# Score tiles of two and three PSUM banks by turns in a fused attention and expert-attention kernel

## The chip, the cores and the metric

The kernel runs on one NeuronCore of a Trainium2 chip. The metric is the device time of one execution in microseconds. The kernel before takes 320.8 us (median of three runs, 320.77 to 320.80). The profile is of one execution with a span of 319.3 us.

Engine names in the profile: PE is TensorE (PEld its weight loads), DVE is VectorE, ACT is ScalarE, POOL is GpSimd, SP issues the transfers.

## What is computed

An attention with a soft cap on its scores, then, on its output, an attention layer of four experts with a gate that picks two of them for each token. Cut to what matters:

```python
# B = 8 batches, 12 heads, S = 448 tokens, 64 columns per head
scores = q @ k.T / sqrt(64)
scores = cap * tanh(scores / cap)              # cap = 30
attn   = softmax(scores)
x      = (attn @ v), heads side by side        # (8, 448, 768)

for e in range(4):                             # experts, causal
    a_e  = softmax(causal(x @ wq[e] @ (x @ wk[e]).T / sqrt(64)))
    y_e  = a_e @ (x @ wv[e]) @ wo[e]
out = sum over the two best experts of a token (logits x @ w_gate) of weight * y_e
```

So each of the 8 x 12 heads has 448 x 448 scores that pass through a tanh and then an exp. Both run on ScalarE.

## The kernel before

Heads are worked on in 48 pairs. The scores of a pair lie transposed: keys on partitions, queries along the row. 448 keys are three blocks of 128 and a tail of 64; the tails of the two heads share one block, so a pair has seven blocks of 128 x 448 scores: one tail block, and three blocks for each head. The first 43 pairs are handled whole; the last five (the last pairs of the last batch) are handled in two halves of tokens ("A" of 256 and "B" of 192 tokens) so that the end of the last batch can overlap.

[...]one block fills one bank (448 of its 512 columns). Scores have two tiles of two banks, used by turns; everything else that TensorE writes (transposes, attention times values, projections, output) takes one of four single banks.

```python
ps_aux   = tile_pool(name="ps_aux", bufs=4, space=PSUM)      # single banks
ps_score = tile_pool(name="ps_score", bufs=2, space=PSUM)    # [128, 2, 512] f32 each
...
HALF = (1, 2, 2, 2)                    # blocks of a whole pair in its four tanh operations

def fill(p, i):                        # scores of part i of pair p, on TensorE
    qt, kt = qkt[p]
    sc = ps_score.tile([128, 2, 512], f32, name=f"s{i}_{p}", tag="score")
    if i == 0:                         # the tail block of both heads
        nc.tensor.matmul(sc[:, 0, 0:S], kt[:, 0:128], qt, start=True, stop=True)
    else:                              # block i of each head: 64 rows of the array each
        for g in range(2):
            r = slice(64 * g, 64 * (g + 1))
            nc.tensor.matmul(sc[:, g, 0:S], kt[r, 128 * i : 128 * (i + 1)], qt[r, :],
                             start=True, stop=True)
    score[(p, i)] = sc

def tanh(u, i):                        # ScalarE, from PSUM to y in SBUF (f16)
    ...
    nc.scalar.activation(dst, src, AF.Tanh, scale=isc / capf)

def expo(u):                           # ScalarE, the whole pair (7 * 448 columns) at once
    nc.scalar.activation(pt[:, 0:n], y.pop(u)[:, 0:n], AF.Exp, scale=capf)
```

The order on ScalarE is a fixed program. For pair i it is: first tanh of pair i, exp of pair i-1, then the other tanh operations of pair i. In some pairs the expert attention of an earlier batch adds two exps of its own ("X", names sB and pBs), which use score tiles too:

```python
XAT = [(3, 5)] * 5 + [(2, 4), (2, 3), (3, 4)]      # in which pairs of the next batch
for i, u in enumerate(UNITS):
    t = [("T", u, k) for k in range(2 if isinstance(u, tuple) else 4)]
    e = [("E", UNITS[i - 1])] if i else []
    x = [("X", *EXPB[i], g) ...] if i in EXPB else []
    if i in (1, 2):
        prog += e + t
    elif isinstance(u, tuple):                     # half pairs at the end
        prog += t[0:1] + e + x + t[1:]
    else:
        prog += t[0:1] + e + x[0:1] + t[1:2] + x[1:2] + t[2:4]
```

While the kernel is built, a small planner (`Plan`) goes through this program, keeps estimated clocks of PE, VectorE and ScalarE, and puts the other TensorE work between the score fills: transposes of q and k ("tr", tile tps), attention times values (pv), its transpose (xt, tile xtp), and for each batch the query and key projections (qps, kps), values (vps), expert attention (pvB), its transposes (otp) and output projections (wops). Its list `aux` has one entry per single bank: the time at which it comes free. Matrix multiplications without use ("dummy") fill gaps of TensorE in the first pairs.

At the end `last_batch` gives the score banks back, opens them as single banks (`ps_tail`, four), and orders what is left with a list scheduler (`Graph`) over both pools.

Of the kernel before, what the change touches and what calls it, by code (L numbers as in the profile page):

```python
# [10 lines left out]
f32 = mybir.dt.float32  # L11
f16 = mybir.dt.float16
AF = mybir.ActivationFunctionType
# [4 lines left out]
class Plan:  # L18
# [6 lines left out]
    def __init__(self):  # L25
        self.pe = self.dve = self.act = 0.0
        self.done = {}

        self.aux = [0.0] * 4
        self.opened = set()  # L30
        self.work = []

# [207 lines left out]
def kernel(  # L240
# [13 lines left out]
    nc = tc.nc  # L254

    B, H, S, Dh = q.shape
# [17 lines left out]
    xp = ctx.enter_context(tc.tile_pool(name="xp", bufs=2))  # L274
    bp = ctx.enter_context(tc.tile_pool(name="bp", bufs=2))
    outp = ctx.enter_context(tc.tile_pool(name="outp", bufs=8))
    ps_aux = ctx.enter_context(tc.tile_pool(name="ps_aux", bufs=4, space=bass.MemoryType.PSUM))
    scores = ctx.enter_context(ExitStack())
    ps_score = scores.enter_context(
        tc.tile_pool(name="ps_score", bufs=2, space=bass.MemoryType.PSUM)  # L280
    )

    ctx.enter_context(tc.manual_schedule())
# [154 lines left out]

    HALF = (1, 2, 2, 2)


    CUT = 256
# [4 lines left out]
    score = {}  # L449

    def fill_part(u, i):

        p, h = u
        qt, kt = qkt[p]
        x = slice(*TOK[h])
        n = x.stop - x.start
        sc = ps_score.tile([128, 2, 512], f32, name=f"s{i}{h}_{p}", tag="score")
# [12 lines left out]
    def fill(p, i):  # L470
        if isinstance(p, tuple):
            return fill_part(p, i)
        qt, kt = qkt[p]
        sc = ps_score.tile([128, 2, 512], f32, name=f"s{i}_{p}", tag="score")
        if i == 0:
            nc.tensor.matmul(sc[:, 0, 0:S], kt[:, 0:128], qt, start=True, stop=True)  # L476
        else:
            for g in range(2):
                r = slice(64 * g, 64 * (g + 1))
                nc.tensor.matmul(  # L480
                    sc[:, g, 0:S], kt[r, 128 * i : 128 * (i + 1)], qt[r, :],
                    start=True, stop=True,
                )
        score[(p, i)] = sc

    y = {}
# [2 lines left out]
    def tanh(u, i):  # L489
        p, h = u if isinstance(u, tuple) else (u, "")  # L490
        if i == 0:
            y[u] = actp.tile([128, 7 * S], f16, name=f"y{h}_{p}", tag="y", bufs=2)
        sc = score.pop((u, i))
        if not h:
            o, n = sum(HALF[0:i]), HALF[i]
            parts = [(o * S, sc[:, 0:n, 0:S], n)]
        else:
            n = TOK[h][1] - TOK[h][0]
            if i == 0:
                parts = [(0, sc[:, :, 0 : 2 * n], 2)]  # L500
            elif 2 * n == 512:
                parts = [(4 * n, sc.rearrange("p b n -> p (b n)")[:, 0 : 3 * n], 1)]
            else:
                parts = [(4 * n, sc[:, 0, 0 : 2 * n], 1), (6 * n, sc[:, 1, 0:n], 1)]
        for o, src, k in parts:
            w = src.shape[-1]
            dst = y[u][:, o : o + k * w]
            if k > 1 or len(src.shape) > 2:
                dst = dst.rearrange("p (k w) -> p k w", w=w)
            nc.scalar.activation(dst, src, AF.Tanh, scale=isc / capf)  # L510
# [8 lines left out]
    def prob(p, w, j, g):  # L519

        h = "AB"[w >= CUT]
        if (p, h) in pr:
            lo, hi = TOK[h]
            i = (4 if j == 0 else 4 + g + (j == 3) if j > 2 else j - 1 + 2 * g)
            o = (hi - lo) * i + w - lo
            return pr[p, h][:, o : o + 128]
        o = S * (0 if j == 0 else 2 * j - 1 + g) + w
        return pr[p][:, o : o + 128]

    xt = {}  # L530
# [96 lines left out]
    st = {b: {} for b in range(B)}  # L627
# [125 lines left out]
    def b_fill(b, r, g):  # L753
        s = st[b]
        qe = s["qe", r]
        ke = s["ke", r]
        sc = ps_score.tile([128, 1024], f32, name=f"sB{g}_{b}_{r}", tag="score")

        def block(e, o, ko, n, to):

            h = slice(64 * e, 64 * (e + 1))
            nc.tensor.matmul(  # L762
                sc[to : to + n, o : o + S - ko], ke[h, ko : ko + n], qe[h, ko:S], start=True,
                stop=True,
            )
# [136 lines left out]
    plan = Plan()  # L902
# [68 lines left out]
        loads += [("o", wo2[e // 2][e % 2 * Dh : (e % 2 + 1) * Dh, :], moe_wo[e])]  # L971


    XAT = [(3, 5)] * 5 + [(2, 4), (2, 3), (3, 4)]
    EXPB = {HP * (b + 1) + o: (b, r) for b in range(B) for r, o in enumerate(XAT[b])}

    prog = []
    for i, u in enumerate(UNITS):  # L980
        t = [("T", u, k) for k in range(2 if isinstance(u, tuple) else 4)]
        e = [("E", UNITS[i - 1])] if i else []
        x = [("X", *EXPB[i], g) for g in range(1 if i >= NP else 2)] if i in EXPB else []
        prog.append(("S", i))
        if i in (1, 2):
            prog += e + t
        elif isinstance(u, tuple):
            prog += t[0:1] + e + x + t[1:]
        else:
            prog += t[0:1] + e + x[0:1] + t[1:2] + x[1:2] + t[2:4]  # L990
    prog += [("S", len(UNITS)), ("E", UNITS[-1])]
    reads = [o for o in prog if o[0] in "TX"]
    where = [i for i, o in enumerate(prog) if o[0] in "TX"]
# [4 lines left out]
    def dur(o):  # L998
        if o[0] == "S":
            return 0.0  # L1000
        if o[0] == "X":
            return 0.7 if o[1] == B - 1 else 0.9
        n = S
        if isinstance(o[1], tuple):
            n = TOK[o[1][1]][1] - TOK[o[1][1]][0]
        if o[0] == "E":
            return 0.08 + 0.00084 * 7 * n
        if n < S:
            return 0.05 + 0.00084 * n * (4, 3)[o[2]] + 0.04 * (o[2] == 1 and n < 256)
        return 0.055 + 0.373 * HALF[o[2]]  # L1010

    def fill_dep(o):
        if o[0] == "T":
# [5 lines left out]
    def do_fill():  # L1019
        nonlocal nfill  # L1020
        o = reads[nfill]
        rel = ends[nfill - 2] + 0.15 if nfill >= 2 else 0.0
        cost = 0.36 if o[0] == "X" or o[2] or isinstance(o[1], tuple) else 0.19
# [15 lines left out]
    t = 0.0  # L1039
# [185 lines left out]


    def l_fill(b, r, _):
        sc = ps_score.tile([128, 2, 512], f32, name=f"sLA_{r}", tag="score")
        o = 0
        for _, k0, q0, q1 in BANKS["A", r][0]:  # L1230
            for e in range(2):
                h = slice(64 * e, 64 * (e + 1))
                nc.tensor.matmul(
                    sc[:, e, o : o + q1 - q0], part_of(1, r, h, k0, k0 + 128),
                    part_of(0, r, h, q0, q1), start=True, stop=True,
                )
            o += q1 - q0
        st[b]["sc", r] = sc

    def l_exp(b, r, _):  # L1240
# [3 lines left out]
        nc.scalar.activation(  # L1244
            dst.rearrange("p (e n) -> p e n", e=2), st[b].pop(("sc", r))[:, :, 0:384], AF.Exp,
            scale=isc,
        )
        for e in range(2):
# [6 lines left out]
    def last_batch():  # L1255


        p, b = NP - 1, B - 1
        c = b - 1
        s, sc = st[b], st[c]  # L1260
        for k in [("v", c, 3), *[("k", c, r) for r in range(2)], ("vl", 0), *plan.opened]:
            plan.force(k)
        while ngate < B - (("lgA",) not in plan.done):
            gate_exp(True)
# [2 lines left out]
        scores.close()  # L1267
        nc.gpsimd.memset(pL[:, :, 320:384], 0.0)
        ps_tail = ctx.enter_context(
            tc.tile_pool(name="ps_tail", bufs=4, space=bass.MemoryType.PSUM)  # L1270
        )
        t3 = plan.done["T", UNITS[-1], 1]
        G = Graph(
            dict(PE=plan.pe, DVE=plan.dve, ACT=plan.act, SP=plan.act, DMA=plan.act),
            dict(aux=[(0.0, t) for t in plan.aux], tail=[(0.0, t3)] * 4),
        )

        BR, BA, BW, BX = 0.0, 0.0, -5.0, 0.0
# [127 lines left out]
        n = S - CUT  # L1406
# [263 lines left out]
```

## Time and profile before

| | value |
|---|---|
| time, median of 3 | 320.8 us |
| span of the profiled execution | 319.3 us |
| ScalarE busy | 306.8 us (96%) |
| TensorE busy | 284.9 us (89%) |
| VectorE busy | 216.8 us (68%) |
| mean granted TensorE clock | 0.987 |
| first tanh starts | 7.29 us |
| last exp of a half pair starts | 302.31 us |

A row of the groups has the line in the kernel, the engine, the operation with its output and input tiles and shapes, then the busy time and the mean duration of one, and last the idle time of the engine just before such operations with what ended it. Busy time is counted once where operations overlap; a mean duration is the whole of one operation, its overlap with neighbours too. A row of the waits has the engine and tile that waited, what it waited for, and then the total in us, the number of waits and the longest.

### The profile page before, as it was taken

The numbers are of one execution on the slowest core, as the hardware profiler recorded it, in microseconds if no ns is written. First come the engines' busy times: TensorE is split into PE (matmuls) and PEld (weight loads), VectorE is DVE, ScalarE is ACT, GpSimd is POOL, SyncE is SP. The second block draws the span as 40 slices with busy tenths as digits, with TensorE's granted clock in tenths as the row PEclk, the third lists the DMA queues.
The fourth block names the chain that finished last, engine by engine and source line by source line (L and its number), as shares of the span: only waits on it lengthen the run. The fifth ranks groups of instructions, "written<-read, shape, count | busy, mean of one in ns | idle before, by whom it ended". The sixth has DMA issues, their size and how long they took to land.

```text
span 319.3 us, 9111 instructions
## 1 busy us (share of the span) xinstructions
PE 284.9 (89%) x3445; PEld 179.6 (56%) x3445; DVE 216.8 (68%) x762; ACT 306.8 (96%) x312; POOL 157.1 (49%) x480
## 2 busy tenths in 40 slices
PE   7887879988999889997799899997999879989994
PEld 2454445655565655566556564655655655556762
DVE  4444446686686877678866876767856976577574
ACT  3999999999999999999999999999999999999973
POOL 4586999947607299865805386082905200220200
PEclk9999999999999999999999979999899999999999
DMA  7699999999026999576083945586012102020134
GB/s 163 173 216 241 211 225 214 223 216 230 4 101 170 257 243 275 148 214 161 13 242 95 257 95 150 169 218 157 3 52 99 27 2 102 0 77 2 52 123 175
DMA packets 65404, 46.22 MB, mean 145 GB/s; under 512 B 26000, under 2 KB 61968, under 8 KB 65360
## 3 DMA queue, kind: packets, MB, share of 16 engines
q1 hardware_dynamic: 54064, 43.28, 53.0%
q0 software_dynamic: 10512, 1.58, 7.1%
q10 hardware_dynamic: 784, 0.77, 0.8%
q8 instruction: 27, 0.44, 0.6%
q14 instruction: 17, 0.14, 0.2%
HBM read 36.19 MB, written 11.01 MB: 148 GB/s over the span
## 4 chain that ended last, share of the span: by engine, by line
ACT 78%; PE 12%; issue 7%; DMA 1%; DVE 1%; DVEq 0%; POOL 0%; ACTq 0%; POOLq 0%
ACT y L510 36%; ACT p L516 30%; ACT pBs L781 8%; PE wops L863 2%; PE vps L640 2%; DMA qf<-in_q_dram 1%; ACT yB L510 1%; PE pv L550 1%; PE qps L724 1%; ACT yA L510 1%; PE kps L724 1%; PE qkB L1171 1%; ACT pB L516 1%; PE pv L544 1%; ACT pBs L1479 0%
## 5 line engine op out<-in xcount | busy, mean ns | idle before, releaser
L510 ACT ACTIVATE y<-s 128x896 f16<-128x896 f32 (+1 forms) x172 | 135.5, 934 | 0.6 <-PE s L476 0.5
L516 ACT ACTIVATE p<-y 128x3136 f16<-128x3136 f16 x43 | 125.7, 2922 | 0.1
L789 POOL TENSOR_SCALAR_AFFINE_SELECT pBs<-pBs 128x128 f16<-128x128 f16 (+1 forms) x112 | 28.2, 277 | 103.5 <-ACT pBs L781 102.2
L550 PE MATMUL pv<-v16s,p 128*128 128x65 f16 x1032 | 55.0, 194 | 0.0
L480 PE MATMUL s<-qt,kt 64*128 64x448 f16 x258 | 46.5, 362 | 9.0 <-ACT y L510 6.8
L550 PEld LDWEIGHTS <-p 128*128 128x128 f16 x1032 | 46.6, 98 | 3.6 <-issue 0.4
L544 PE MATMUL pv<-vtzs,p 128*128 128x130 f16 x172 | 38.8, 225 | 9.0 <-ACT p L516 6.7
L559 DVE RECIPROCAL rc<-pv 128x4 f32<-128x4 f32 x96 | 17.3, 180 | 38.0 <-PE pv L550 36.8
L563 DVE TENSOR_TENSOR xk<-pv,rc 128x256 f16<-128x256 f32 x96 | 40.7, 424 | 3.2
L370 DVE COPY ob<-wops 128x384 f32<-128x384 f32 (+1 forms) x55 | 30.5, 554 | 6.3 <-PE wops L863 5.7
L544 PEld LDWEIGHTS <-p 128*128 128x128 f16 x172 | 16.7, 97 | 27.7 <-ACT p L516 15.5
L480 PEld LDWEIGHTS <-kt 64*128 64x128 f16 x258 | 15.7, 93 | 28.3 <-issue 21.5
L781 ACT ACTIVATE pBs<-sB 128x960 f16<-128x960 f32 (+1 forms) x28 | 30.9, 1116 | 0.5 <-PE sB L762 0.5
L863 PE MATMUL wops<-wo,oT 128*128 128x384 f16 x128 | 30.4, 327 | 0.6 <-DVE oT L370 0.4
L385 POOL CAST q<-qf 112x512 f16<-112x512 f32 x46 | 28.1, 611 | 4.7 <-DMA qf<-in_q_dram 2.8
L640 PE MATMUL vps<-wvg,xT 128*128 128x260 f16 (+1 forms) x192 | 29.6, 275 | 0.0
L399 POOL CAST v16s<-vf 128x384 f16<-128x384 f32 x48 | 24.4, 507 | 6.0 <-DMA vf<-in_v_dram 3.2
L386 POOL CAST k<-kf 128x384 f16<-128x384 f32 x48 | 24.3, 506 | 3.6 <-DMA kf<-in_k_dram 3.6
L370 DVE COPY xT<-xtp 128x448 f16<-128x448 f16 (+2 forms) x52 | 19.1, 368 | 10.2 <-PE xtp L585 8.8
L404 POOL CAST vtzs<-vtf 64x64 f16<-64x64 f32 x96 | 22.5, 234 | 4.7 <-DMA vtf<-in_v_dram 2.0
L431 DVE COPY qt<-tps 128x384 f16<-128x384 f16 x48 | 16.9, 351 | 8.9 <-PE tps L421 8.5
L391 POOL CAST ktzs<-ktf 64x64 f16<-64x64 f32 x92 | 21.4, 232 | 2.8
(178 smaller groups left out, 544.6 us busy)
## 6 DMA issues: line engine op xcount, KB each, us to landing
qf<-in_q_dram SPq DMA_DIRECT2D x22, 448.0 KB, 6.2
out_dram<-ob SPq DMA_DIRECT2D x23, 384.0 KB, 2.3
kf<-in_k_dram SPq DMA_DIRECT2D x22, 384.0 KB, 6.5
vf<-in_v_dram SPq DMA_DIRECT2D x22, 384.0 KB, 6.1
out_dram<-ob SPq DMA_DIRECT2D x8, 192.0 KB, 2.8
ktf<-in_k_dram SPq DMA_DIRECT2D x44, 32.0 KB, 5.6
vtf<-in_v_dram SPq DMA_DIRECT2D x44, 32.0 KB, 5.4
kf<-in_k_dram SPq DMA_DIRECT2D x4, 192.0 KB, 3.5
```

The lines of the kernel that those rows point to most:

```text
L370: (nc.scalar.copy if act else nc.vector.tensor_copy)(dst, src)
L385: eng.tensor_copy(q16, qf.rearrange("p h (c d) -> p c h d", c=QC))
L480: nc.tensor.matmul(sc[:, g, 0:S], kt[r, 128 * i : 128 * (i + 1)], qt[r, :], start=True, stop=True,)
L510: nc.scalar.activation(dst, src, AF.Tanh, scale=isc / capf)
L516: nc.scalar.activation(pt[:, 0:n], y.pop(u)[:, 0:n], AF.Exp, scale=capf)
L544: nc.tensor.matmul(pv[:, n, :, :], prob(p, w, 0, 0), vtz[p % 12], start=(n == 0), stop=False, skip_group_check=True,)
L550: nc.tensor.matmul(pv[:, n, g, :], prob(p, w, j, g), v16[p % 12][:, g, j - 1, :], start=False, stop=(j == KC), skip_group_check=True,)
L563: nc.vector.tensor_tensor(xt[p][:, 2 * i : 2 * i + 2, :, :], pv[:, :, :, 0:Dh], rc.broadcast_to((128, 2, 2, Dh)), ALU.mult,)
L640: nc.tensor.matmul(ps, xT[b][:, j, w : w + 128], wvg[:, j, 0 : ps.shape[1]], start=(j == 0 and first), stop=(j == NDC - 1), skip_group_che ...
L781: nc.scalar.activation(pb[:, o0 : o0 + n], st[b].pop(("sc", r, g))[:, 0:n], AF.Exp, scale=isc)
L789: nc.gpsimd.affine_select(out=blk, in_=blk, compare_op=ALU.is_ge, fill=0.0, base=0, pattern=[[1, n]], channel_multiplier=-1,)
L863: nc.tensor.matmul(ps, st[b]["oT", r][:, w : w + 128], wo2[r][:, f * (D // 2) : (f + 1) * (D // 2)], start=(r == 0), stop=(r == 1),)
```

## The change

A pair's seven blocks are read by three tanh operations (2, 2 and 3 blocks) instead of four (1, 2, 2, 2). For this one of the two score tiles has three banks; the other keeps two. All reads of score tiles (tanh of pairs and half pairs, expert exps) use the two tiles by turns. Which of the three tanh operations takes the tail block, and so three blocks, follows from which tile falls to it: the second of a pair as a rule, the third where a pair without expert exps begins on the three-bank tile. The place of the expert exps in a pair, and in one batch the pair, are set to fit. One of the single banks is given up for it; the planner's list has three entries. At the end the five score banks all become single banks (`ps_tail`, five).

It is for fewer ScalarE operations on the same scores. The diff, cut to its core:

```diff
-        self.aux = [0.0] * 4
+        self.aux = [0.0] * 3
...
-    ps_aux = ctx.enter_context(tc.tile_pool(name="ps_aux", bufs=4, space=bass.MemoryType.PSUM))
+    ps_aux = ctx.enter_context(tc.tile_pool(name="ps_aux", bufs=3, space=bass.MemoryType.PSUM))
...
-        tc.tile_pool(name="ps_score", bufs=2, space=bass.MemoryType.PSUM)
+        tc.tile_pool(name="ps_score", bufs=1, space=bass.MemoryType.PSUM)
...
-    HALF = (1, 2, 2, 2)
+    TAILAT = {0: 1}
+    nscore = 0
+
+    def score_tile(name):
+        nonlocal nscore
+        i = nscore % 2
+        nscore += 1
+        return ps_score.tile([128, 2 + i, 512], f32, name=name, tag=f"score{i}")
+
+    def chunks(p, i):
+        return ([0] if TAILAT[p] == i else []) + [i + 1] * 2
...
-        sc = ps_score.tile([128, 2, 512], f32, name=f"s{i}_{p}", tag="score")
-        if i == 0:
-            nc.tensor.matmul(sc[:, 0, 0:S], kt[:, 0:128], qt, start=True, stop=True)
-        else:
-            for g in range(2):
-                ...
+        sc = score_tile(f"s{i}_{p}")
+        for n, c in enumerate(chunks(p, i)):
+            if c == 0:
+                nc.tensor.matmul(sc[:, 0, 0:S], kt[:, 0:128], qt, start=True, stop=True)
+                continue
+            g = n % 2 ^ (TAILAT[p] == i)
+            r = slice(64 * g, 64 * (g + 1))
+            nc.tensor.matmul(
+                sc[:, n, 0:S], kt[r, 128 * c : 128 * (c + 1)], qt[r, :],
+                start=True, stop=True,
+            )
...
-    XAT = [(3, 5)] * 5 + [(2, 4), (2, 3), (3, 4)]
+    XAT = [(3, 5)] * 5 + [(2, 4), (2, 4), (3, 4)]
...
-        t = [("T", u, k) for k in range(2 if isinstance(u, tuple) else 4)]
+        t = [("T", u, k) for k in range(2 if isinstance(u, tuple) else 3)]
...
+        big = nread % 2
+        nread += len(t + x)
...
+        elif big:
+            prog += t[0:1] + e + x[0:1] + t[1:2] + x[1:2] + t[2:3]
         else:
-            prog += t[0:1] + e + x[0:1] + t[1:2] + x[1:2] + t[2:4]
+            prog += t[0:1] + e + t[1:2] + x + t[2:3]
+        if not isinstance(u, tuple):
+            TAILAT[u] = 2 if big and not x else 1
...
-        for k in [("v", c, 3), *[("k", c, r) for r in range(2)], ("vl", 0), *plan.opened]:
+        for k in [("v", c, 3), ("xt", p - 3, "B"), *[("k", c, r) for r in range(2)], ("vl", 0), *plan.opened]:
             plan.force(k)
...
-            tc.tile_pool(name="ps_tail", bufs=4, space=bass.MemoryType.PSUM)
+            tc.tile_pool(name="ps_tail", bufs=5, space=bass.MemoryType.PSUM)
...
-            dict(aux=[(0.0, t) for t in plan.aux], tail=[(0.0, t3)] * 4),
+            dict(aux=[(0.0, t) for t in plan.aux], tail=[(0.0, t3)] * 5),
```

The rest of the diff lets the exp's reader and the planner's costs follow the new places of the blocks.

More of the change, by code (lines that the diff above doesn't have):

```diff
@@ L437, in a_tr, with y_of @@
         qkt[p] = (qt, kt)
-    HALF = (1, 2, 2, 2)
+    TAILAT = {0: 1}
[7 more added lines that the diff above has]
+        return ([0] if TAILAT[p] == i else []) + [i + 1] * 2
+    def y_of(p, j):
+        if j == 0:
+            return 2 * TAILAT[p]
+        return 2 * (j - 1) + (TAILAT[p] <= j - 1)
     CUT = 256
@@ L456, in fill_part @@
         n = x.stop - x.start
-        sc = ps_score.tile([128, 2, 512], f32, name=f"s{i}{h}_{p}", tag="score")
+        sc = score_tile(f"s{i}{h}_{p}")
         if i:
@@ L473, in fill @@
         qt, kt = qkt[p]
-        sc = ps_score.tile([128, 2, 512], f32, name=f"s{i}_{p}", tag="score")
-        if i == 0:
-            nc.tensor.matmul(sc[:, 0, 0:S], kt[:, 0:128], qt, start=True, stop=True)
-        else:
-            for g in range(2):
[L479 to L483, printed above, removed]
+        sc = score_tile(f"s{i}_{p}")
[9 more added lines that the diff above has]
+            )
         score[(p, i)] = sc
@@ L494, in tanh @@
         if not h:
-            o, n = sum(HALF[0:i]), HALF[i]
+            cs = chunks(p, i)
+            o, n = y_of(p, cs[0]), len(cs)
             parts = [(o * S, sc[:, 0:n, 0:S], n)]
@@ L499, in tanh @@
             if i == 0:
-                parts = [(0, sc[:, :, 0 : 2 * n], 2)]
+                parts = [(0, sc[:, 0:2, 0 : 2 * n], 2)]
             elif 2 * n == 512:
@@ L526, in prob @@
             return pr[p, h][:, o : o + 128]
-        o = S * (0 if j == 0 else 2 * j - 1 + g) + w
+        o = S * (y_of(p, j) + g) + w
         return pr[p][:, o : o + 128]
@@ L756, in b_fill @@
         ke = s["ke", r]
-        sc = ps_score.tile([128, 1024], f32, name=f"sB{g}_{b}_{r}", tag="score")
+        sc = score_tile(f"sB{g}_{b}_{r}").rearrange("p b n -> p (b n)")
         def block(e, o, ko, n, to):
@@ L971 @@
         loads += [("o", wo2[e // 2][e % 2 * Dh : (e % 2 + 1) * Dh, :], moe_wo[e])]
-    XAT = [(3, 5)] * 5 + [(2, 4), (2, 3), (3, 4)]
+    XAT = [(3, 5)] * 5 + [(2, 4), (2, 4), (3, 4)]
     EXPB = {HP * (b + 1) + o: (b, r) for b in range(B) for r, o in enumerate(XAT[b])}
     prog = []
+    nread = 0
     for i, u in enumerate(UNITS):
-        t = [("T", u, k) for k in range(2 if isinstance(u, tuple) else 4)]
+        t = [("T", u, k) for k in range(2 if isinstance(u, tuple) else 3)]
         e = [("E", UNITS[i - 1])] if i else []
         x = [("X", *EXPB[i], g) for g in range(1 if i >= NP else 2)] if i in EXPB else []
+        big = nread % 2
+        nread += len(t + x)
         prog.append(("S", i))
@@ L1009, in dur @@
             return 0.05 + 0.00084 * n * (4, 3)[o[2]] + 0.04 * (o[2] == 1 and n < 256)
-        return 0.055 + 0.373 * HALF[o[2]]
+        return 0.055 + 0.373 * len(chunks(o[1], o[2]))
     def fill_dep(o):
@@ L1022, in do_fill @@
         rel = ends[nfill - 2] + 0.15 if nfill >= 2 else 0.0
-        cost = 0.36 if o[0] == "X" or o[2] or isinstance(o[1], tuple) else 0.19
+        cost = 0.36
+        if o[0] == "T" and not isinstance(o[1], tuple) and TAILAT[o[1]] == o[2]:
+            cost += 0.19
         for d in fill_dep(o):
@@ L1227, in l_fill @@
     def l_fill(b, r, _):
-        sc = ps_score.tile([128, 2, 512], f32, name=f"sLA_{r}", tag="score")
+        sc = score_tile(f"sLA_{r}")
         o = 0
@@ L1244, in l_exp @@
         nc.scalar.activation(
-            dst.rearrange("p (e n) -> p e n", e=2), st[b].pop(("sc", r))[:, :, 0:384], AF.Exp,
+            dst.rearrange("p (e n) -> p e n", e=2), st[b].pop(("sc", r))[:, 0:2, 0:384], AF.Exp,
             scale=isc,
```

## Prediction

> **What bounds the kernel now.** I read the page's busy table first, then the groups of instructions, then what each engine waited for, then the order of time on ScalarE, and last the chain of work in the final 20 us.
>
> ```profile
> PE 284.9 (89%) x3445; PEld 179.6 (56%) x3445; DVE 216.8 (68%) x762; ACT 306.8 (96%) x312; POOL 157.1 (49%) x480
> ...
> L510 ACT ACTIVATE y<-s 128x896 f16<-128x896 f32 (+1 forms) x172 | 135.5, 934 | 0.6 <-PE s L476 0.5
> L516 ACT ACTIVATE p<-y 128x3136 f16<-128x3136 f16 x43 | 125.7, 2922 | 0.1
> ```
>
> ScalarE (ACT) is busy 96% of the span. Its two big groups are the tanh operations (172 of them, 4 for each of 43 head pairs) and one exp per pair; the last column says that ScalarE hardly ever stood idle before either (0.6 and 0.1 us in all). A view that lists ScalarE's waits between 7.3 and 298 us has only two lines:
>
> ```profile
> ACT y L510 <- PE s L476: 0.5, 1, 0.5
> ACT pBs L781 <- PE sB L762: 0.5, 1, 0.5
> ```
>
> So for 290 us ScalarE never stops: whatever is taken from its instruction stream there is taken from the time, as long as TensorE still fills the score tiles in time. What one tanh costs must be read from starts, not from the durations, because neighbours overlap. The timeline of ScalarE, asked in narrow windows so that it doesn't merge the pieces (columns: start, duration, instruction):
>
> ```profile
> 102.57 1.08 ACT L510 ACTIVATE y<-s 128x896 f16<-128x896 f32 x1
> 103.37 1.09 ACT L510 ACTIVATE y<-s 128x896 f16<-128x896 f32 x1
> 104.17 1.10 ACT L510 ACTIVATE y<-s 128x896 f16<-128x896 f32 x1
> 104.98 0.72 ACT L510 ACTIVATE y<-s 128x448 f16<-128x448 f32 x1
> 105.41 3.00 ACT L516 ACTIVATE p<-y 128x3136 f16<-128x3136 f16 x1
> ```
>
> From start to start a tanh of 896 columns takes 0.80 us and one of 448 takes 0.43. The 448 further columns cost 0.37 us (0.83 ns each), so a single operation carries 0.43 - 0.37 = 0.06 us that doesn't depend on its size; with 0.80 - 0.747 it is 0.053. I take 0.056.
>
> The end is another stage. The chain of waits, in order of time, is on TensorE (PE) without a break from 296 to 307 us, not on ScalarE:
>
> ```profile
> 303.33 0.65 PE wops L863 x4
> 304.03 0.18 PE pv L550 x6
> 304.21 0.17 PE qkB L1171 x2
> 304.44 0.18 PE pv L550 x6
> 304.62 0.11 PE xtp L608 x2
> 304.73 0.65 PE wops L863 x4
> 305.38 0.17 PE qkB L1171 x2
> 305.55 0.33 PE wops L863 x2
> ```
>
> The reader is to see that output projections of the batch before (wops) stand between the steps of the last batch (pv, xtp, qkB): TensorE works off a backlog there. The busy time by stretches says the same: from 296 to 304 us PE is busy 7.95 of 8.00 us, from 304 to 308.2 it is 4.20 of 4.20, from 308.2 to 312 only 3.23 of 3.80, and after that 3.06 of 7.30. Any work pushed into the stretch up to 308 costs its full length; later some of it hides.
>
> **What the skill says.** The Trainium skill, "Perfetto Trace Analysis", section Optimizing Scalar/DVE Operations, gives about 51 ns of fixed access time for a ScalarE operation on PSUM, and says that grouping into larger operations helps where the engine is saturated. The trace agrees: 53 to 60 ns, on an engine at 96%. "ScalarE: Activation LUTs", section What ACT_TABLE_LOAD costs, gives 0.833 ns per element whatever the function; the trace has 0.83. "PSUM — Partial Sum Buffer", section Specifications (TRN2), gives 8 banks of 512 f32 per partition, and its four rules let a matmul write one bank only. So a pair's seven blocks of 448 scores remain seven banks' worth of matmul output, and the budget is 2+2+4 banks before and 2+3+3 after; the trace cannot show banks, but its score shapes (448 and 896) are one and two blocks. "Perfetto Trace Analysis", section Optimization Strategy, names repeated gaps on the engine that should be saturated as a sign of too little PSUM; the two waits above say that the kernel before has none, and that is what three single banks could change.
>
> **The change part by part.**
>
> *Three tanh operations per pair.* The sizes go from 448+896+896+896 to 896+896+1344 in some order. Elements are the same 3136. One fixed cost per pair goes: 43 x 0.056 = 2.4 us, all on ScalarE and all in its saturated stage. A look at the two built instruction orders confirms the count: 172 against 129 tanh operations on whole pairs. The ten half-pair units at the end (25 operations), the exps and the expert exps (28 and 2) keep their number and size.
>
> *Score fills on TensorE.* Same seven matmuls per pair (301 in both orders), grouped 2+2+3. Nothing is gained or lost in time, but the deadlines move. Two tiles by turns mean that a tile can be refilled from the end of its own read until the other's read ends. In the kernel before, the tight refills of a pair are the fourth read and the next pair's first, each behind a tanh of 0.80 us; the others lie behind the exp of some 2.7 us. After, only the next pair's first refill (two blocks) lies behind the third tanh, of 0.80 us or 1.17 (0.80 + 0.37 for three blocks). Two 64-row score matmuls take 0.30 us from start to start in the trace (7.18 to 7.48), so this fits as before, and one tight refill per pair is less than two. I count zero for it.
>
> *Three instead of four single banks.* All other TensorE results (transposes, pv, projections, values) use them. A pv unit holds a bank from its first matmul to the end of the division: in the trace 126.94 (first matmul) to 128.16 + 0.42 = 128.58, 1.6 us; in the window of 125 to 150 us a transpose unit runs from 126.51 to 127.62 + 0.41 = 128.03, 1.5 us. Per pair there are 4 such units, and per batch of six pairs 22 more (4 query/key, 4 value, 4 expert pv, 2 transposes, 8 output projections), 7.7 per pair. A pair takes 5.56 us (the chain has the tanh groups of two plain pairs at 30.36 and 35.92), and some 0.6 us more on average for the 28 expert exps (28 x 0.86 / 43). So 7.7 x 1.5 / 6.1 = 1.9 banks are held on average, an estimate from these rows. Three banks hold that, but with much less room for a late VectorE, whose evacuations are already 77% busy in that window (19.26 of 25 us). TensorE's order is fixed when the kernel is built, so each wait for a bank delays the fill behind it. I allow 0.2 us of new ScalarE waits.
>
> *The start.* The first tanh now needs two matmuls before it instead of one. Two 64-row matmuls take about as long as one full one; I take 0.1 us.
>
> *The tail.* ScalarE's stage ends earlier, so TensorE has less time before it, and the order shows more left over. Behind the last score fill of the last half pair, the kernel before has 12 value, 28 projection (wops) and no gate matmuls (lgA) there; the changed one has 15, 32 and 12. By the chain's rows, three value matmuls are 0.33 us, the 12 gate matmuls 0.39 and four wops 0.65: 1.4 us more in all. Before the first score matmul of the last half (sLB), the stretch where PE has no gap, it adds 0.33 + 0.39 and moves six expert pv (about 0.35) and two transposes (0.1) behind it: +0.25 us. The rest, about 1.1 us, falls between the last exps and the stores, where PE has gaps; I charge half, 0.5. The tail's bank pools stay eight in all (3+5 for 4+4). Tail: +0.75 us.
>
> Sum: -2.4 + 0.2 + 0.1 + 0.75 = -1.35 us, so 320.8 - 1.35 = **319.4 us**.
>
> **The rivals.**
>
> *Full gain.* The tail's order comes from a search over many orders and might be as short as before. Then 320.8 - 2.4 + 0.1 = 318.5 us, or below it where the second tight refill had cost something. Against it: the leftover count, and PE's unbroken chain up to 307 us.
>
> *TensorE becomes the bound through the banks.* PE is already busy 24.15 of 25 us from 225 to 250 us, and the page counts pipelined matmuls, so not all of the rest is room. If each of the 43 pairs got one wait of 0.06 us, the gain would be gone (320.8); at 0.15 us it would be slower by 4 us (324.8). For it: a fixed order, three banks, VectorE at 77%. Against it: the waits of PE in the steady stage are mostly for ScalarE (score tiles 6.8 us, exps 6.7 us), that is PE runs ahead; waits for VectorE are single ones of 0.3 to 1.0 us.
>
> *A larger operation that costs more than its columns.* If a tanh over three banks ran at a worse rate than 0.83 ns per column, the saving would shrink; 448 and 896 lie on one line, so I give this little.
>
> **Range and chances.** The 2.4 us are firm to 0.2. The tail can move by 1 us either way and the banks can only cost: 317.8 to 321.6 us. Faster by over 2% means under 314.4, which asks for more than twice what the fixed costs hold: 0.02. Slower by over 2% means over 327.2, 0.2 us of new wait in every pair: 0.04.
>
> **What would show it.** Right: 129 tanh operations in the whole-pair group, the 1344 form 1.15 to 1.20 us from start to start, a plain pair some 0.055 us shorter than 5.56; ScalarE's waits from 7.3 to 298 us under 1.5 us; the last exp of a half pair (at 302.31 us before) about 2.2 us earlier; and from there to the end about 0.7 us longer. Wrong: repeated ScalarE waits for score fills with PE waiting for VectorE ahead of them, which is the bank rival; or a tail that is shorter than before, which is the full gain.

## The result and the profile after

The changed kernel takes 319.58 us (median of five runs, 319.42 to 320.07) against 320.80 before; the ratio is 0.996, with a 95% interval of 0.9946 to 0.9975. It is 1.2 us faster, where 1.4 was predicted.

The busy table of the changed kernel and its two large groups, from its page:

```profile
PE 283.6 (89%) x3436; PEld 174.9 (55%) x3436; DVE 217.1 (68%) x760; ACT 304.7 (96%) x271; POOL 157.9 (50%) x480
...
L532 ACT ACTIVATE y<-s 128x896 f16<-128x896 f32 x129 | 132.6, 1149 | 0.5 <-PE s L501 0.5
L538 ACT ACTIVATE p<-y 128x3136 f16<-128x3136 f16 x43 | 125.7, 2924 | 0.1
```

There are 129 tanh operations instead of 172, and ScalarE is still 96% busy. (The group mixes the two shapes here; it names the first.) The mean duration has grown from 934 to 1149 ns and says little by itself; starts say more. ScalarE's timeline in narrow windows, a plain pair of the changed kernel:

```profile
102.32 1.40 ACT L532 ACTIVATE y<-s 128x1344 f16<-128x1344 f32 x1
103.49 1.04 ACT L532 ACTIVATE y<-s 128x896 f16<-128x896 f32 x1
104.29 1.05 ACT L532 ACTIVATE y<-s 128x896 f16<-128x896 f32 x1
105.09 2.96 ACT L538 ACTIVATE p<-y 128x3136 f16<-128x3136 f16 x1
```

The three-block operation takes 1.17 us from start to start, the others 0.80: three steps of 2.77 us in the place of four of 2.84 (102.57 to 105.41 before). ScalarE's waits between the start of the first tanh and 299 us:

```profile
ACT y L532 <- PE s L501: 0.5, 1, 0.5
ACT yA L532 <- PE s0A L484: 0.2, 1, 0.2
```

The first belongs to the start of the kernel, as it does before. So three single banks do not starve ScalarE. The end is different. ScalarE's timeline around the last exp of a half pair, which starts at 299.56 us (302.31 before):

```profile
299.56 1.32 ACT L538 ACTIVATE pB<-yB 128x1344 f16<-128x1344 f16 x1
...
304.48 1.03 ACT L370 CAST qkB<-qkB 128x384 f16<-128x384 f32 x2 [0.61 <-PE qkB L1202]
305.40 0.21 ACT L696 ACTIVATE eexpB<-lgB 128x8 f32<-128x8 f32 x1
305.68 1.02 ACT L370 COPY ob<-wops 128x384 f32<-128x384 f32 x2
306.72 0.87 ACT L1510 ACTIVATE pBs<-sLB 128x384 f16<-128x384 f32 x2
```

The copies of the last half's queries and keys (qkB) start 4.92 us after that exp, as before (307.22 against 302.31). But then evacuations (ob) of projections of the batch before stand ahead of the last half's scores, and their first exp comes 7.16 us after the last half-pair exp, in the kernel before 6.28 (308.59 against 302.31):

```profile
307.22 0.96 ACT L370 CAST qkB<-qkB 128x384 f16<-128x384 f32 x2 [0.84 <-PE qkB L1171]
308.41 0.21 ACT L674 ACTIVATE eexpB<-lgB 128x8 f32<-128x8 f32 x1 [0.23 <-DVE lgB L1402]
308.59 0.87 ACT L1479 ACTIVATE pBs<-sLB 128x384 f16<-128x384 f32 x2
```

That is the timeline of the kernel before; here nothing of an older batch stands between. The delay arises on TensorE, however. Its timeline, first of the kernel before and then of the changed one, at the last score fill of a half pair (s1B) and at the last half's scores (sLB):

```profile
299.72 0.24 PE L459 MATMUL s1B<-qt,kt 128*128 128x192 f16 x1
...
308.22 0.34 PE L1453 MATMUL sLB<-qkB,qkA 64*128 64x192 f16 x4
```

```profile
297.41 0.25 PE L479 MATMUL s1B<-qt,kt 128*128 128x192 f16 x1
...
305.69 0.49 PE L885 MATMUL wops<-wo,oT 128*128 128x384 f16 x2
306.02 0.27 PE L662 MATMUL vps<-wvg,xT 128*128 128x256 f16 x1
306.22 0.34 PE L1484 MATMUL sLB<-qkB,qkA 64*128 64x192 f16 x4
```

The score matmuls start 6.66 us after the exp instead of 5.91, which is 0.75 of the 0.88 us. From them to their first exp it is 0.50 us instead of 0.37, so the two evacuations that ScalarE does just ahead cost 0.13 us at most. TensorE's busy time from the exp to the end of the last output evacuation, before and after (columns: stretch, length, busy time of PE, PEld, DVE, ACT and POOL, then the granted clock, the busy share of the transfer engines and GB/s):

```profile
302.31:315.99 13.68, 12.13 (x152) 8.19 (x149) 9.70 (x41) 10.37 (x22) 0.34 (x2) 1.00 0.35 131
```

```profile
299.56:314.45 14.89, 13.18 (x182) 9.55 (x178) 10.83 (x48) 11.04 (x25) 0.35 (x2) 1.00 0.37 137
```

TensorE has 1.05 us more to do in a stretch that is 1.2 us longer.

For what follows a run's span is cut in four: the start, until the first tanh; the *stage*, from the first tanh's start to the start of the last half-pair exp; the *tail*, from there to the end of the last output evacuation (ob); and the *stores*, from there to the end. The start is not shown: it lies between 7.0 and 7.7 us with no pattern in the kernels, since it hangs on the first transfer.

| kernel | stage us | tail us | stores us | median us | ratio to before, 95% interval |
|---|---|---|---|---|---|
| before | 295.02 | 13.69 | 3.28 | 320.80 | |
| after | 291.85 | 14.89 | 3.90 | 319.58 | 0.9946 to 0.9975 |
| e1, triple split | 294.26 | 14.89 | 3.92 | 322.05 | 1.0011 to 1.0037 |
| e2, before, three banks | 294.67 | 14.91 | 4.26 | 323.42 | 1.0049 to 1.0089 |
| e3, after, no leftover projections | 291.71 | 13.12 | 4.18 | 317.93 | 0.9880 to 0.9926 |
| e4, before, no leftover projections | 295.32 | 12.40 | 4.24 | 320.92 | 0.9988 to 1.0022 |
| e5, fourth bank for half pairs | 292.37 | 14.05 | 3.92 | 319.47 | 0.9937 to 0.9968 |
| e6, other tail order | 291.72 | 14.84 | 3.90 | 319.49 | 0.9927 to 0.9962 |
| e7, e5 with longer search | 292.39 | 14.19 | 4.05 | 319.62 | 0.9934 to 0.9966 |
| e8, after again | 291.70 | 14.89 | 4.01 | 319.52 | 0.9932 to 0.9965 |
| e9, e5 with pools apart | 295.44 | 14.05 | 3.93 | 320.93 | 0.9973 to 1.0002 |
| e10, less TensorE work | 291.91 | 15.34 | 3.68 | 320.34 | 0.9962 to 0.9986 |
| e11, no projection of batch 5 | 292.07 | 14.15 | 4.40 | 319.39 | 0.9941 to 0.9973 |
| e12, e9 with the bank later | 291.73 | 13.92 | 4.32 | 319.19 | 0.9916 to 0.9967 |

The first three columns are of the profiled execution, the last two of the timed runs, each against runs of the kernel before on the same chip. The ratio, and not the median, compares rows, since the kernel before took 320.80 to 321.38 us by the median on the chips used. Stage and tail repeat well (after and e8: 291.85 and 291.70, 14.89 twice). So do the stores where the tail has the same order (after, e1 and e8: 3.90, 3.92 and 4.01; e5 and e9: 3.92 and 3.93); between different orders they lie between 3.28 and 4.40 us. The stretches from the last evacuation on show what they consist of, in the kernel before and in the changed one:

```profile
315.99:318.00 2.01, 0.00 (x0) 0.00 (x0) 0.00 (x1) 0.00 (x0) 0.00 (x0) 1.00 0.92 294
```

```profile
314.45:317.10 2.65, 0.00 (x0) 0.00 (x0) 0.01 (x1) 0.00 (x0) 0.00 (x0) 1.00 0.89 281
```

For 2.01 and 2.65 us the transfer engines are busy with what is left (294 GB/s x 2.01 us = 0.59 MB, 281 x 2.65 = 0.74 MB), then come 1.27 and 1.25 us without a transfer. The first of the last six stores is issued 2.91 us ahead of the end of the last evacuation before and 2.36 us after, so that the closer end leaves more to move; this was not tested by itself. The expectations below speak of a tail that includes the stores; the text gives both.

So by the profiles the change takes 3.17 us from the stage and adds 1.20 to the tail and 0.62 to the stores.

### The profile page after: what moved, and what is told of

It reads as the page before. It is cut to its first block, busy times and chain, and to the rows that moved or that the text cites. A ratio compares the mean times of both kernels' runs of the same rounds, so it can differ in the third digit from the quotient of the medians.

```text
span 318.4 us, 9095 instructions
## 1 busy us (share of the span) xinstructions
PE 283.6 (89%) x3436; PEld 174.9 (55%) x3436; DVE 217.1 (68%) x760; ACT 304.7 (96%) x271; POOL 157.9 (50%) x480
## 4 chain that ended last, share of the span: by engine, by line
ACT 71%; PE 18%; issue 7%; DMA 1%; DVE 1%; POOL 1%; POOLq 0%; ACTq 0%
ACT y L532 30%; ACT p L538 28%; ACT pBs L803 7%; PE wops L885 3%; PE vps L662 2%; ACT yB L532 2%; PE kps L746 2%; PE pv L572 2%; PE qps L746 2%; PE s L501 2%; DMA qf<-in_q_dram 1%; PE sB L784 1%; ACT pB L538 1%; PE pv L566 1%; ACT pBs L1510 1%
## 5 line engine op out<-in xcount | busy, mean ns | idle before, releaser
L532 ACT ACTIVATE y<-s 128x896 f16<-128x896 f32 x129 | 132.6, 1149 | 0.5 <-PE s L501 0.5
L572 PE MATMUL pv<-v16s,p 128*128 128x65 f16 x1032 | 53.0, 193 | 0.0
L572 PEld LDWEIGHTS <-p 128*128 128x128 f16 x1032 | 45.4, 97 | 1.4
L370 DVE COPY ob<-wops 128x384 f32<-128x384 f32 (+1 forms) x53 | 29.4, 554 | 6.3 <-PE wops L885 5.6
L566 PEld LDWEIGHTS <-p 128*128 128x128 f16 x172 | 16.6, 97 | 29.1 <-ACT p L538 16.4
```

The lines of the kernel that those rows point to most:

```text
L370: (nc.scalar.copy if act else nc.vector.tensor_copy)(dst, src)
L566: nc.tensor.matmul(pv[:, n, :, :], prob(p, w, 0, 0), vtz[p % 12], start=(n == 0), stop=False, skip_group_check=True,)
L572: nc.tensor.matmul(pv[:, n, g, :], prob(p, w, j, g), v16[p % 12][:, g, j - 1, :], start=False, stop=(j == KC), skip_group_check=True,)
```

## The experiments

**What an operation costs (e1).**

```diff
+            if k == 3:
+                nc.scalar.activation(dst[:, 0:2], src[:, 0:2], AF.Tanh, scale=isc / capf)
+                nc.scalar.activation(dst[:, 2:3], src[:, 2:3], AF.Tanh, scale=isc / capf)
+                continue
             nc.scalar.activation(dst, src, AF.Tanh, scale=isc / capf)
```

> The kernel after, with its 43 tanh operations over three blocks each cut into one over two blocks and one over one block. Score tiles, banks, the order on TensorE and VectorE and the tail stay as they are. If the saving is the fixed part of an operation (0.048 to 0.051 us by the starts in the two traces), it comes back 43 times: 319.6 + 43 x 0.05 = 321.7 us, and the stage from the first tanh to the last exp of a half pair grows from 291.9 to 294.0 us. If the saving came from the new order of score tiles instead (fewer late fills behind one tight refill a pair), this stays near 319.6 (under 320.3).

The stage grew by 2.41 us, the tail stayed to the hundredth, and the median is 322.05 us. The 43 operations put back cost 2.41 / 43 = 0.056 us each. The same pair in narrow windows of ScalarE's timeline:

```profile
102.47 1.09 ACT L533 ACTIVATE y<-s 128x896 f16<-128x896 f32 x1
103.26 0.72 ACT L534 ACTIVATE y<-s 128x448 f16<-128x448 f32 x1
103.69 1.11 ACT L536 ACTIVATE y<-s 128x896 f16<-128x896 f32 x1
```

Two blocks and one take 1.22 us from 102.47 to 103.69, where the triple took 1.17: 0.05 us for the split itself. Where the rest of the 0.056 lies is not traced. So most of these 2.41 us is the fixed part of an operation; the new order of the tiles, which e1 keeps, is not their source.

**What a single bank costs (e2).** The kernel before, with one bank less and all else as it was:

```diff
-        self.aux = [0.0] * 4
+        self.aux = [0.0] * 3
...
-    ps_aux = ctx.enter_context(tc.tile_pool(name="ps_aux", bufs=4, space=bass.MemoryType.PSUM))
+    ps_aux = ctx.enter_context(tc.tile_pool(name="ps_aux", bufs=3, space=bass.MemoryType.PSUM))
...
-            tc.tile_pool(name="ps_tail", bufs=4, space=bass.MemoryType.PSUM)
+            tc.tile_pool(name="ps_tail", bufs=5, space=bass.MemoryType.PSUM)
...
-            dict(aux=[(0.0, t) for t in plan.aux], tail=[(0.0, t3)] * 4),
+            dict(aux=[(0.0, t) for t in plan.aux], tail=[(0.0, t3)] * 5),
```

> The kernel before, with its four tanh operations per pair and two score tiles of two banks, but three single banks instead of four (one bank lies idle until the tail, where five score banks come free). Theory: three banks are enough while ScalarE is the bound, so the stage from the first tanh to the last exp of a half pair stays 295.0 us within 0.3; but TensorE gets less done beside it and the tail grows from 17.0 to 17.5 to 18.5 us: 321.3 to 322.3 us in all. Rival, the longer tail has nothing to do with the lost bank: 320.8 us within 0.3, tail 17.0. Rival, banks starve ScalarE: the stage grows by over 1 us.

The stage did not grow, and the tail went from 13.69 to 14.91 us, which is what the changed kernel has (14.89). The stores went from 3.28 to 4.26 us. The median is 323.42 us, 1.1 us more than the upper end of what was expected. The profiled execution is the fastest of the six (322.55 us, mean granted clock 0.998); four others, granted 0.989 to 0.994, took 323.32 to 323.84 us, and no trace shows where. This is the clearest of the runs: taking one bank away reproduces the whole longer tail without any change to the tanh operations. ScalarE's timeline looks as after, only with four evacuations ahead of the scores' first exp; here too the score matmuls themselves are late on TensorE, 7.46 us after the last half-pair exp (5.91 before). TensorE is busy 13.17 us in that tail (12.13 before), not with more projections (28 wops matmuls are in its tail in both) but with the last batch's own work: 36 matmuls of qkB for 18, 22 of pv for 14, 12 gate matmuls for none. ScalarE's lines:

```profile
307.56 0.89 ACT L370 COPY ob<-wops 64x384 f32<-64x384 f32 x2
308.69 0.91 ACT L370 COPY ob<-wops 128x384 f32<-128x384 f32 x2 [0.23 <-PE wops L863]
309.50 0.88 ACT L1479 ACTIVATE pBs<-sLB 128x384 f16<-128x384 f32 x2
```

With e1 the change comes apart into two: fewer operations, worth 2.4 us, and a lost bank, which costs 1.2 us before the stores and 2.2 with them. They do not add up to all of it (-2.41, -0.35 in the stage of e2 and +2.20 are -0.56, against -1.35 for the change): 0.4 us more is gone from the stage of the changed kernel, and its stores are 0.4 us shorter than those of e2.

**Is it the work left over? (e3, e4)** Both kernels, with the output projections of batch 6 that the planner leaves for the end left out (eight after, six before), their evacuations and stores too. The output lacks those rows.

```diff
-                if ("wo", c, n, f) in left:
-                    d = [[("oT", c, 0), ("oT", c, 1)]]
-                    project(c, n, f, (0,), d)
-            if ("wo", c, n, 1) in left:
-                store(c, n)
+                pass
```

> The kernel after, with the output projections of the last batch but one that are left for the tail left out: all eight, 16 matmuls (16 x 0.163 = 2.6 us of TensorE by the chain's rows), their eight evacuations and their stores. Its output lacks these rows. If the tail is bound by the backlog of TensorE, its length falls from 18.8 us to about 16.5 (not all of the 2.6 us lies on the path), so 317.3 us, and the tail equals that of the kernel before without its leftover to 0.5 us. If the tail is a chain of dependences into which these projections merely fit, it stays within 0.5 us of 18.8.

> The kernel before with the same left out of its tail: here six output projections, 12 matmuls (2.0 us of TensorE), are left there. By the backlog theory the tail falls from 17.0 to about 15.5 us (319.3 us in all), and the two tails without leftovers agree to 0.5 us, but for the 12 gate matmuls that only the kernel after has there (0.4 us). By the rival that the order found for the tail was worse by chance, the tails without leftovers still differ by over 1 us or not at all, without regard to the work left.

With the stores, the tails are 17.30 and 16.64 us: e3 fell by 1.5 us, somewhat less than expected, e4 by only 0.3, a miss, and its time is that of the kernel before (0.9988 to 1.0022). Without the stores, which took 0.96 us longer in e4 than before, the tails fell by 1.77 (14.89 to 13.12) and by 1.29 us (13.69 to 12.40). So the leftover projections lie on the path to the last evacuation in both kernels; that they cost time to the end is shown for the changed one alone. The two tails without them still differ by 0.72 us. TensorE's timeline shows what else is left behind the last half-pair exp in e3 and not in e4: 12 gate matmuls, and 28 matmuls of qkB for 22.

**Is it a matter of chance in the tail's order? (e6, e8)**

```diff
-        rnd = random.Random(1)
+        rnd = random.Random(2)
```

> The kernel after with another starting value for the search that orders the tail; everything up to the tail and the work left in it are the same. If what is left sets the tail, it stays 18.8 within 0.5 us (319.1 to 320.1 us in all). If the order found by chance set it, it may move by 1 us or more either way.

> The kernel after, unchanged, beside the three others on one chip: 319.6 us within 0.5, stage 291.9 us, tail 18.8 us. All theories expect the same.

Another order of the same leftover work gives 14.84 us beside 14.89, and the same total. It is one other order, not many, but the search does not explain 1.2 us. In e6 the first exp of the last half comes 6.59 us after the last half-pair exp, 0.57 sooner than in the kernel after, and the tail is as long. So it is not that exp that sets it; TensorE is busy 13.72 us in that tail.

**A fourth bank where it can be had (e5, e7, e9, e12).** Half pairs and expert exps read two banks at most. From the first half pair on, the third bank of the larger score tile can be a single bank again.

```diff
+        if nfill == half0:                    # first fill of a half pair
+            scores.close()
+            ...                               # two score tiles of two banks, and
+            halves.append(scores.enter_context(
+                tc.tile_pool(name="ps_half", bufs=1, space=bass.MemoryType.PSUM)
+            ))
+        if nfill == half0 + 2:
+            plan.aux.append((ends[nfill - 2] + 0.2, "half"))
```

> The kernel after, but once the half-pair units begin (they and the expert exps read at most two banks) the third bank of the larger score tile is handed over as a fourth single bank for the last 40 us; the tail's order is searched anew over the same eight banks. Theory (three single banks let TensorE do less beside ScalarE, and what is left lengthens the tail): the gate matmuls are no longer left for the tail, and the tail falls from 18.8 to 17.0 to 18.0 us with the ScalarE stage unchanged (291.9, within 0.4): 318.6 to 319.2 us in all. Rival (the tail is longer because the search found a worse order, whatever is left): no reason to fall, 319.6 within 0.5. A stall where the score tiles change hands would show as one ScalarE wait of up to 0.8 us.

> The kernel with the fourth bank for the half pairs, and four times as many tries in the search for the tail's order. By the theory the search adds little: within 0.4 us of the same kernel with the shorter search. By the rival it is faster by 0.5 us or more. Either way this is the version that should beat both kernels: 318.2 to 319.2 us.

The tail fell from 14.89 to 14.05 us (with stores 17.97 for 18.79) and the gate matmuls are no longer in it, but the stage grew by 0.5 us, so that the total is what it was (319.47). ScalarE's waits in e5 show why: closing one pool for both tiles makes the first half-pair fill wait for both.

```profile
ACT yA L541 <- PE s0A L493: 0.7, 2, 0.5
ACT y L541 <- PE s L510: 0.5, 1, 0.5
```

Four times as many tries in the search (e7) brought nothing: 14.19 us.

In e9 the two score tiles got pools of their own, so that only the larger one is closed, and the bank was given to the planner at the first half-pair fill (`nfill == half0`) rather than two fills later.

> As the kernel with a fourth single bank for the half pairs, but the two score tiles lie in pools of their own, and only the three-block tile's pool is closed and opened again, so that the first half-pair fill doesn't wait for both old tiles. If the 0.5 us wait for the first half-pair fill was all that ate the gain, the ScalarE stage returns from 292.4 to 291.8 us, the tail stays near 18.0, and the time is 318.7 to 319.1 us. If the bank brings nothing by itself, it is 319.5 as the kernel after.

It went the other way: 320.93 us, with runs from 319.8 to 322.3, and a stage of 295.44 us in the profiled one, which is the slowest of them. TensorE's wait in e9 at the change of tiles, its busy time by stretches there (columns as above), and ScalarE's wait:

```profile
PE s0A L494 <- ACT y L542: 2.2, 1, 2.2
```

```profile
261.90:264.00 2.10, 0.16 (x3) 0.09 (x1) 1.02 (x4) 2.10 (x3) 0.00 (x0) 1.00 0.00 0
264.00:267.40 3.40, 3.13 (x30) 1.91 (x29) 0.81 (x3) 3.40 (x4) 0.00 (x0) 0.51 0.00 0
```

```profile
ACT pBs L813 <- PE sB L794: 2.1, 1, 2.1
```

With the bank offered too early the planner put nothing between two fills where the kernel after has transposes, a projection and pv. TensorE stood idle for 2.2 us, was then granted half its clock for 3.4 us, and ScalarE waited 2.1 us for scores some 10 us later. The other large wait of that run (1.4 us at 15.9 us) also follows a stretch at half clock, which begins at 11.5 us; e9 changes nothing there. In e12 the bank is handed over one fill later:

```diff
-            plan.aux.append((ends[nfill - 2] + 0.2, "half"))
+        if nfill == half0 + 1:
+            plan.aux.append((ends[nfill - 3] + 0.2, "half"))
```

> As the version with its own pool for the three-block tile, but the freed bank is given to the planner after the first half-pair fill instead of ahead of it. The run before had TensorE idle for 2.2 us at that place, its clock at one half for 3.4 us after it, and ScalarE waiting 2.1 us; here transposes, a projection and pv stand there again as in the kernel after. Expected: no ScalarE wait over 0.3 us at the change of tiles, stage 291.8 us within 0.3, tail 17.9 to 18.2 us: 318.6 to 319.1 us in all, 0.5 us under the kernel after. If the fourth bank brings nothing, 319.5.

Stage 291.73 us, tail 13.92, so 0.97 us of the 1.20 that the lost bank had cost came back; with the stores the tail is 18.24 for 18.79 us, 0.55 of 1.82. The time is 319.19 us, a little above what was expected, because the stores took 4.32 us. The ratio to before is 0.9942 (0.9916 to 0.9967). Its interval overlaps that of the kernel after (0.9932 to 0.9965 in e8), so that it beats it is likely by the profile and not settled by the times.

**TensorE's total, or what is left? (e10, e11)** The changed kernel, with half of batch 5's output projections left out (e10), and with all of them left out (e11); the output of that batch is partial or missing.

```diff
 # e10: one of two matmuls for b == 5
-        b_wo_mm(b, n, f, st[b]["wo", n, f], (0, 1))
+        if b == 5:
+            b_wo_half(b, n, f, st[b]["wo", n, f])
+        else:
+            b_wo_mm(b, n, f, st[b]["wo", n, f], (0, 1))
...
 # e11
-                plan.add(("wo", b, n, f), 0.33, 0.5, d, due, b_wo, b, n, f)
+                if b != 5:
+                    plan.add(("wo", b, n, f), 0.33, 0.5, d, due, b_wo, b, n, f)
```

> The kernel after with half of each output projection of batch 5 left out (one of two matmuls, 8 in all, 1.3 us of TensorE; its output for that batch is a part of the sum), and the planner told so. The orders show that the planner now leaves more for the tail, not less: 12 value matmuls of the last batch's first half and 4 transposes on top of what the kernel after leaves. If what is left sets the tail, it grows by about 1 us to 19.5 to 20.3 us (320.3 to 321.1 us in all), though TensorE has less work as a whole. If TensorE's total work sets it, the tail falls to about 17.5 (318.3 us).

> The kernel after with all output projections of batch 5 left out (16 matmuls, 2.6 us of TensorE, eight evacuations, its stores; its output for that batch is missing). The orders show the same projections of batch 6 left for the tail, but no gate matmuls and three fewer value matmuls (0.7 us less of TensorE). If what is left sets the tail, it falls by 0.5 to 0.9 us to about 18.1 (318.9 us in all). If TensorE's total work sets it, it falls by the whole 1.8 us to 17.0.

e10: with stores 19.02 us instead of the 19.5 to 20.3 expected; without them 15.34, 0.45 us longer than after. It has less TensorE work in all and no shorter tail, so the total does not set it; the growth is half of what the count of leftover matmuls promised, with stores a quarter. e11: without stores 14.15 us, 0.74 shorter than after, as much as the work taken out of the tail (0.7); with them 18.55, only 0.24 shorter, since its stores took 4.40 us. The total work would have taken 1.8 us off. Both speak against the total, and in sign for what is left; the size fits in e11 alone, and only up to the last evacuation.

## Why the prediction was right, and where by luck

1. *The saving per operation* was put at 43 x 0.056 = 2.4 us. e1 measures 2.41, of which 43 x 0.05 = 2.15 us is the fixed part. That a tanh over three blocks keeps the rate, which two sizes could not show, is now measured: 1.17 us for 0.80 + 0.37. The 51 ns that the Trainium skill ("Perfetto Trace Analysis", section Optimizing Scalar/DVE Operations) gives for ScalarE on PSUM is what the split shows: 1.22 against 1.17 us.
2. *The score fills* were counted as zero. That missed 0.76 us of gain: the stage fell by 3.17 us. The sum of start-to-start times of the whole-pair tanh operations falls from 123.39 to 120.60 us, 0.38 more than e1 accounts for. That need not be the new order of the fills: three late starts of the kernel before, 0.48 us together, lie at 184.8, 185.7 and 222.8 us, at two stretches with TensorE at half clock. The profile after has none ahead of its end; e2, which has none there either, comes to 123.08 us with the old order. A wait for the expert exps near the end of the stage is gone (0.5 us in the list of the kernel before; e2 still has it), and the last gate exp (0.10 us) has moved behind the stage. Smaller terms both ways make up the rest. None of this was tested by itself. The clock is in the times too: of the 28 runs of the kernel before beside e8, the eight at a mean granted clock of 1.0 took 320.67 us by the median, the other twenty (0.981 to 0.995) 321.43. The six of e8 had 0.997 or more and took 319.52, so that at like clock the gain there is 1.15 us.
3. *The banks* were allowed 0.2 us of new ScalarE waits. There are none: the waits that followed a score fill went from 1.0 to 0.7 us. The rival "TensorE becomes the bound through the banks" is wrong for the stage. The bank's cost is real, but it is paid at the end.
4. *The start* was given 0.1 us; the runs do not resolve it (7.0 to 7.7 us). In the two profiles compared here it is 0.42 us later after (7.71 for 7.29), of which the matmuls have no share: two of 64 rows take 0.30 us to the next start (7.30 to 7.60), the full one before took 0.29 (6.89 to 7.18).
5. *The tail* was given +0.75 us, stores included; it is +1.82. This is the term that was mis-sized. The mechanism, more TensorE work left over, holds, and both sums of the prediction come out when they are counted as it did, from the last score fill of the last half pair: to the last half's scores 8.81 us for 8.50 (+0.31, predicted +0.25), from there to the last evacuation 8.23 for 7.77 (+0.46, predicted +0.5). Two things were left out. That fill starts 2.15 us ahead of the last exp instead of 2.59, so 0.44 us more of the work falls behind the stage: 0.10 for the gate exp, the rest because TensorE is later than ScalarE (the fill starts 0.50 us after the start of the exp before the last one, instead of 0.16). And the closer end leaves more of the stores to move, 0.62 us.

Without the start, the profiled executions give -3.17 + 1.82 = -1.35 us for a predicted -1.45 (with it the spans differ by 0.9, the medians by 1.2). That they agree so closely is luck: the stage was off by 0.97 us and the tail by 1.07, in opposite directions. What is shown: the cost per operation (e1), that one bank less alone makes the tail as long (e2), that leftover work lies on the path (e3 to the end; e4 and e11 to the last evacuation), and that a bank given back for the last 40 us takes most of it off before the stores, and a third with them (e12). What stays open is how the planner comes to leave more with three banks; e10 shows that it isn't simply TensorE's total.

## What to carry to other kernels

On an engine that never stops, count operations and read their fixed cost from start to start; here merging two reads of PSUM saved about 0.05 us each time. A buffer given up for it may cost nothing where the engine is saturated and still be paid for at the end, as work that no longer fitted beside it: compare what stands behind the bound stage in the two orders, on every engine, and how closely the last stores follow one another. If a buffer is needed only in one phase, give it back for the other.

## What the runs showed of the hardware

- An operation on ScalarE can start late without any idle time in the profile, since its duration overlaps the next one's start by about 0.23 us (a tanh of 896 columns lasts 1.03 us and the next starts after 0.80). The 129 such operations of the kernel before take 0.797 us by the median and 0.814 by the mean: 129 x 0.017 = 2.2 us of late starts, while the groups of instructions, kept apart by shape, list 0.0 us of idle time before them. Only starts show them.
- After TensorE had been idle for 2.2 us its granted clock was 0.51 for 3.4 us (e9). The profile of the kernel before has two such stretches, each behind several shorter gaps (1.5 and 0.45 us; 0.9, 0.2, 0.4 and 0.2 us), and that of the kernel after has none before its end. The length of the gaps alone does not decide it: in e4 gaps of 1.47 and 0.45 us at the same place were followed by no such stretch. The first of those of the kernel before (columns as above):

```profile
184.90:188.30 3.40, 3.20 (x39) 2.39 (x40) 1.61 (x7) 3.33 (x5) 3.00 (x10) 0.50 0.48 118
```

- The last six stores were issued within 2.9 us in the kernel before and 2.4 us in the one after. From the last evacuation on the 16 transfer engines then had a busy share of 0.92 for 2.01 us and of 0.89 for 2.65 us, and the program ended 1.27 and 1.25 us after the last of these transfers.
